# Moving an inverse square root from POOL to ScalarE in a fused attention-and-MLP kernel, with later weight loads, deeper input buffers and every engine in emission order

## The chip, the cores and the metric

One core of one Trainium2 chip. The metric is device microseconds of one execution. The kernel before took 673.85 us, the median of 3 runs (670.53 to 674.61).

## The reference, cut to what matters

```python
# q, k, v: (8 batches, 12 heads, 448 rows, 64)
def rmsnorm(x, g):
    return x / np.sqrt(np.mean(x * x, -1, keepdims=True) + 1e-06) * g
scores = np.matmul(rmsnorm(q, g_q), rmsnorm(k, g_k).transpose(0, 1, 3, 2)) / 8
attn = softmax(scores);  x = np.matmul(attn, v)        # to (3584, 768)
h = x @ w_in                                            # (3584, 2048)
out = (h * np.clip(h + 3, 0, 6) / 6) @ w_out            # (3584, 768)
```

The change concerns the inverse square root inside `rmsnorm`, one value per row and head, and the order of everything around it.

## The kernel before

Two heads form a pair, so there are 48 pairs P, six per batch. Each head's 448 rows are 384 rows plus a remainder of 64; the remainders of q and k of two batches are prepared together, at batches 0, 2, 4 and 6. A pair is loaded, prepared (squares, sums, inverse root, scaling), transposed on PE, scored, and multiplied by v. The MLP of a batch follows one batch later (h) and two batches later (y), so that PE always has something to mix in. The pools `ps_...` hold tiles of PSUM, the memory that PE writes its results to; one such tile is called a bank here.

```python
def rstd_of(ssq, n):                                   # inverse root, on POOL
    nc.gpsimd.tensor_scalar(ms[:], ssq, 1.0 / D, 1e-6, A_MULT, A_ADD)
    nc.gpsimd.tensor_tensor(out=rs[:], in0=ms[:], in1=npow[:, 0:n], op=A_POW)

def prep_pair(P):
    nc.gpsimd.tensor_tensor(out=sq[:], in0=qk_flat, in1=qk_flat, op=A_MULT)
    nc.vector.tensor_reduce(out=ssq[:], in_=sq..., axis=AX_X, op=A_ADD)
    rs = rstd_of(ssq[:], 4 * NT)
    for i in range(2):
        nc.gpsimd.tensor_tensor(out=qks[:, i]..., in0=qk[:, i]..., in1=rs..., op=A_MULT)
    nc.gpsimd.tensor_copy(out=va..., in_=vf...)

def prep_rest(b):                                      # remainder of batches b, b + 1
    for i in range(2):                                 # q, then k
        nc.gpsimd.tensor_tensor(out=sq[:], in0=src, in1=src, op=A_MULT)
        nc.vector.tensor_reduce(out=ssq[:], ...)
        rs = rstd_of(ssq[:], H)
        nc.gpsimd.tensor_tensor(out=qks[:, i], in0=qkr[:, i], in1=rs..., op=A_MULT)
# ... cut ...
ps_T = pool("ps_T", 1, space=PSUM)    # all transposes
ps_S = pool("ps_S", 3, space=PSUM)    # scores
ps_M = pool("ps_M", 2, space=PSUM)    # h and y share two banks
# ... cut ...
def att_items(P):                     # one attention step; fn's are called in this order
    items = [(0.0, lambda: load_step(P + 4)), (0.0, lambda: prep_step(P + 3)),
             (0.36, lambda: trans_step(P + 2))]
    # then scores of P+1 mixed with the v products of P, then the transpose of x
def h_items(G):                       # a group of 6 matmuls in two halves
    return [(c, lambda f=f, p=p: h_part(G, f, p)) for f in range(NFT) for p in range(2)]
# after half 2: ReLU on ScalarE, gating on VectorE; then the bank is free
```

Before, a scheduler arranges the recorded instructions on each engine. "Emission order" below means that each engine's instructions stay in the order in which the program calls them.

Of the kernel before, what the change touches and what calls it, by code (L numbers as in the profile page):

```python
# [10 lines left out]
BF16 = mybir.dt.bfloat16  # L11
A_MULT = mybir.AluOpType.mult
A_ADD = mybir.AluOpType.add
A_POW = mybir.AluOpType.pow
A_MIN = mybir.AluOpType.min
EXP = mybir.ActivationFunctionType.Exp
RELU = mybir.ActivationFunctionType.Relu
AX_X = mybir.AxisListType.X
# [4 lines left out]
def kernel(  # L23
# [33 lines left out]
    gq_t = const.tile([128, 1], FP32, name="gq_t")  # L57
    gk_t = const.tile([128, 1], FP32, name="gk_t")
    for a in range(2):
        nc.sync.dma_start(out=gq_t[a * 64:(a + 1) * 64, :], in_=g_q.rearrange("(p o) -> p o", o=1))  # L60
        nc.sync.dma_start(out=gk_t[a * 64:(a + 1) * 64, :], in_=g_k.rearrange("(p o) -> p o", o=1))
    mask = const.tile([128, 2], FP32, name="mask")
    nc.gpsimd.memset(mask[:], 0.0)
    nc.gpsimd.memset(mask[0:64, 0:1], 1.0)
# [1 line left out]
    gprime = const.tile([128, 1], FP32, name="gprime")  # L66
    nc.vector.tensor_mul(gprime[:], gq_t[:], gk_t[:])
    gmask = const.tile([128, 2], FP32, name="gmask")
    nc.vector.tensor_scalar(gmask[:], mask[:], gprime[:], 1.0 / 8.0, A_MULT, A_MULT)
    half_c = const.tile([128, 1], FP32, name="half_c")  # L70
    nc.gpsimd.memset(half_c[:], 0.5)
    zero_c = const.tile([128, 1], FP32, name="zero_c")
    nc.gpsimd.memset(zero_c[:], 0.0)
    npow = const.tile([128, 24], FP32, name="npow")
    nc.gpsimd.memset(npow[:], -0.5)

    w_in_sb = const.tile([128, NKT, DFF], BF16, name="w_in_sb")
    w_out_sb = const.tile([128, NFT, DM], BF16, name="w_out_sb")
# [17 lines left out]
        vbd_ring.append(t)  # L96


    qk_pool = pool("qk_pool", 4)
    v_pool = pool("v_pool", 3)  # L100
    sq_pool = pool("sq_pool", 2)
    st_pool = pool("st_pool", 4)
    qks_pool = pool("qks_pool", 4)
# [19 lines left out]
    st = {}  # L123


    def rstd_of(ssq, n):
        ms = st_pool.tile([128, n], FP32, name="ms", tag="ms")
        nc.gpsimd.tensor_scalar(ms[:], ssq, 1.0 / D, 1e-6, A_MULT, A_ADD)  # L128
        rs = st_pool.tile([128, n], FP32, name="rs", tag="rs")
        nc.gpsimd.tensor_tensor(out=rs[:], in0=ms[:], in1=npow[:, 0:n], op=A_POW)  # L130
        return rs

    def load_pair(P):
        b, j = divmod(P, NPAIR)
# [11 lines left out]
    def prep_pair(P):  # L146
        qk, vf = st.pop(("qk", P)), st.pop(("vf", P))
        sq = sq_pool.tile([128, 4 * NT * D], FP32, name="sq", tag="sq")
        qk_flat = qk[:].rearrange("p a h x -> p (a h x)")
        nc.gpsimd.tensor_tensor(out=sq[:], in0=qk_flat, in1=qk_flat, op=A_MULT)  # L150
        ssq = st_pool.tile([128, 4 * NT], FP32, name="ssq", tag="ssq")
        nc.vector.tensor_reduce(  # L152
            out=ssq[:], in_=sq[:].rearrange("p (n d) -> p n d", d=D), axis=AX_X, op=A_ADD)
        rs = rstd_of(ssq[:], 4 * NT)
        rs4 = rs[:].rearrange("p (a h t) -> p a h t", a=2, h=2)
        qks = qks_pool.tile([128, 2, NT, 2, D], BF16, name="qks")
        for i in range(2):
            nc.gpsimd.tensor_tensor(  # L158
                out=qks[:, i].rearrange("p t h d -> p h t d"),
                in0=qk[:, i].rearrange("p h (t d) -> p h t d", d=D),  # L160
                in1=rs4[:, i].unsqueeze(3).to_broadcast([128, 2, NT, D]),
                op=A_MULT)
        va = va_ring[P % NVA]
        nc.gpsimd.tensor_copy(
            out=va[:, :, :, 0:D], in_=vf[:].rearrange("p h (t d) -> p h t d", d=D))
        st["qks", P] = qks
        st["va", P] = va


    def load_rest(b):  # L170
        qkr = rst_pool.tile([128, 2, H, D], FP32, name="qkr")
        for i, src in enumerate((q, k)):
            for e in range(2):
                nc.sync.dma_start(  # L174
                    out=qkr[e * 64:(e + 1) * 64, i],
                    in_=src[b + e, :, SM:S, :].rearrange("h p d -> p h d"))
        st["qkr", b] = qkr
# [8 lines left out]
    def prep_vrest(b):  # L186
        vr = st.pop(("vr", b))
        vbd = vbd_ring[b % NVB]
        for a in range(2):
            nc.gpsimd.tensor_scalar(  # L190
                vbd[:, :, a * E1:a * E1 + D], vr[:], mask[:, a:a + 1], None, A_MULT)
        st["vbd", b] = vbd

    def prep_rest(b):
        qkr = st.pop(("qkr", b))
        qks = rst_pool.tile([128, 2, H, D], BF16, name="qkrs")
        for i in range(2):
            sq = sq_pool.tile([128, 4 * NT * D], FP32, name="sqr", tag="sq")
            src = qkr[:, i].rearrange("p h d -> p (h d)")
            nc.gpsimd.tensor_tensor(out=sq[:], in0=src, in1=src, op=A_MULT)  # L200
            ssq = st_pool.tile([128, H], FP32, name="ssqr", tag="ssq")
            nc.vector.tensor_reduce(
                out=ssq[:], in_=sq[:].rearrange("p (n d) -> p n d", d=D), axis=AX_X, op=A_ADD)
            rs = rstd_of(ssq[:], H)
            nc.gpsimd.tensor_tensor(  # L205
                out=qks[:, i], in0=qkr[:, i],
                in1=rs[:].unsqueeze(2).to_broadcast([128, H, D]), op=A_MULT)
        st["qkrs", b] = qks
# [44 lines left out]
    def score(P, u):  # L253
        b, j = divmod(P, NPAIR)
        if u == 0:
            st["e", P] = e_pool.tile([128, NU, S], BF16, name="eT")
        if u < 2 * NT:
            a, t = UNITS[u]
            lhsT = st["kp", P][:, a, t * 128:(t + 1) * 128]
        else:  # L260
            lhsT = st["kbd", b][:, j, :]
        ps = ps_S.tile([128, S], FP32, name="s_ps")
        nc.tensor.matmul(out=ps[:], lhsT=lhsT, rhs=st["qT", b][:, j, :], start=True, stop=True)  # L263
        nc.scalar.activation(out=st["e", P][:, u, :], in_=ps[:], func=EXP, bias=zero_c[:], scale=1.0)  # L264
# [117 lines left out]
    def h_items(G):  # L382
        c = 3 * ncol(G) / 2400
        return [(c, lambda f=f, p=p: h_part(G, f, p)) for f in range(NFT) for p in range(2)]
# [5 lines left out]
    def merge(*lists):  # L390
        totals = [sum(c for c, _ in l) or 1.0 for l in lists]
        done = [0.0] * len(lists)
        at = [0] * len(lists)
        res = []
        while True:
            live = [i for i in range(len(lists)) if at[i] < len(lists[i])]
            if not live:
                return res
            i = min(live, key=lambda i: (done[i] + lists[i][at[i]][0] / 2) / totals[i])
            c, fn = lists[i][at[i]]  # L400
            at[i] += 1
            done[i] += c
            res.append((c, fn))
# [4 lines left out]
    def load_step(P):  # L408
        if P >= NP:
            return  # L410
        b, j = divmod(P, NPAIR)
        load_pair(P)
        if j == 0:
            if b % 2 == 0:
                load_rest(b)
            load_vrest(b)

    def prep_step(P):
        if P >= NP:
            return  # L420
        b, j = divmod(P, NPAIR)
        prep_pair(P)
        if j == 0:
            if b % 2 == 0:
                prep_rest(b)
            prep_vrest(b)

    def trans_step(P):
        if P >= NP:
            return  # L430
        b, j = divmod(P, NPAIR)
        trans_pair(P)
        if j == 0 and b % 2 == 0:
            trans_rest(b)

    def att_items(P):
        b, j = divmod(P, NPAIR)
        n = P + 1
        items = [(0.0, lambda: load_step(P + 4)), (0.0, lambda: prep_step(P + 3)),
                 (0.36, lambda: trans_step(P + 2))]  # L440
        sc = [(0.19, lambda u=u: score(n, u)) for u in range(NU)] if n < NP else []
        vs = [(0.3, lambda t=t: av(P, t)) for t in range(NT + 1)]
        items += merge(sc, vs)
        items.append((0.18, lambda: xtrans(P)))
        if b % 2 == 1 and j % 3 == 2:
            items.append((0.18, lambda: xtrans_rest(b, j - 2)))
        return items

    for P in range(4):
        load_step(P)  # L450
    for kt in range(NKT):
        nc.gpsimd.dma_start(out=w_in_sb[:, kt, :], in_=moe_w_in[kt * 128:(kt + 1) * 128, :])
    for P in range(3):
        prep_step(P)
    for ft in range(0, NFT, 4):
        nc.gpsimd.dma_start(
            out=w_out_sb[:, ft:ft + 4, :],
            in_=moe_w_out[ft * 128:(ft + 4) * 128, :].rearrange("(f p) n -> p f n", p=128))
    for P in range(2):
        trans_step(P)  # L460
    for u in range(NU):
        score(0, u)

    for b in range(B):
        att = []
        for j in range(NPAIR):
            att += att_items(b * NPAIR + j)
        mlp = merge(h_items(b - 1) if b >= 1 else [], y_items(b - 2) if b >= 2 else [])
        for _, fn in merge(att, mlp):
            fn()  # L470
    for _, fn in merge(h_items(B - 1), y_items(B - 2)):
        fn()
    for _, fn in y_items(B - 1):
        fn()


# [28 lines left out]
```

## Time and profile before

The stretches below come from the table of windows. Its columns are the stretch, its length, the busy microseconds (and instructions) of PE, PE's weight loads, VectorE (DVE), ScalarE (ACT) and POOL, then PE's granted clock (1.00 is full speed), the mean share of the DMA engines, and GB/s.

```profile
0.00:33.60 33.60, 0.00 (x0) 0.00 (x0) 3.68 (x11) 0.00 (x0) 12.75 (x29) 1.00 0.97 193
33.60:200.00 166.40, 85.39 (x714) 52.57 (x715) 62.86 (x143) 63.53 (x113) 151.84 (x144) 0.80 0.41 98
200.00:500.00 300.00, 245.80 (x1939) 144.14 (x1938) 122.88 (x268) 147.80 (x261) 173.57 (x168) 0.92 0.24 70
500.00:600.00 100.00, 97.83 (x822) 58.69 (x820) 41.73 (x97) 65.19 (x115) 19.51 (x24) 1.00 0.12 39
```

PE does nothing for the first 33.6 us. Then POOL is busy for 91% of the time while PE is half busy at a mean clock of 0.80. From 200 us PE is busy for 82%, and only in the last stretch shown is it busy nearly all the time (98%).

Two groups of POOL's instructions (count, then busy microseconds and mean nanoseconds of one, then POOL's idle time before them):

```profile
L130 POOL TENSOR_TENSOR rs<-ms,npow 128x12 f32<-128x12 f32 x56 | 127.3, 2274 | 3.2
L150 POOL TENSOR_TENSOR sq<-qk 128x768 f32<-128x768 f32 x48 | 70.4, 1466 | 108.3 <-DMA qk<-in_k_dram 107.8
```

The power costs 2274 ns although it works on 12 elements per partition. The squares wait 107.8 us for loads.

From the list of waits of VectorE and of PE (who waited for whom: microseconds, times, longest):

```profile
DVE ssq L152 <- POOL sq L150: 170.8, 44, 11.2
...
PE t_ps L241 <- POOL qks L158: 51.8, 9, 36.1
PE xt_ps L329 <- DVE xn L291: 41.2, 14, 7.0
PE h_ps L349 <- DVE gT_1655 L356: 11.7, 3, 5.2
```

PE waits for the scaled q and k (36.1 of the 51.8 us are the start) and for VectorE's normalised x; in 23 of these 41.2 us VectorE, by its timeline, stood at a sum `ssq` that waited for POOL's squares. Waits of h on gating, over all tiles, add to 43.5 us.

### The profile page before, as it was taken

How to read it: one execution, taken by the hardware profiler on the slowest of the kernel's cores; microseconds unless marked ns; L12 is line 12 of the kernel's file. 1: busy time of each engine (PE TensorE's matmuls, PEld its weight loads, DVE VectorE, ACT ScalarE, POOL GpSimd, SP SyncE). 2: the span in 40 equal slices, each digit the busy share in tenths (PEclk: the TensorE clock that was granted, in tenths of full speed). 3: DMA queues.
4: the chain of work that ended last, by engine and by line, in shares of the span. 5: the costliest groups of instructions: out<-in, count | busy, mean ns of one | idle time of the engine just before them, and what ended most of it. 6: DMA issues, size and time to landing. Idle time of an engine off the chain costs nothing.

```text
span 672.3 us, 9839 instructions
## 1 busy us (share of the span) xinstructions
PE 493.8 (73%) x3848; PEld 290.1 (43%) x3848; DVE 245.9 (37%) x544; ACT 295.9 (44%) x521; POOL 357.7 (53%) x362
## 2 busy tenths in 40 slices
PE   0026354742869767978788868797879999999997
PEld 0013133421545434545454434464545556664454
DVE  0124223533645424334334423334444443433210
ACT  0006142531546434554345335464556666653321
POOL 2499699999796766546355684646455210000000
PEclk9999675877889978998789779999999999999999
DMA  8919733323331331222131212131222110101012
GB/s 154 232 43 198 147 100 85 93 59 83 89 83 49 93 90 53 86 79 61 58 83 49 71 47 71 59 95 60 84 59 71 48 37 25 36 24 36 24 47 72
DMA packets 69647, 50.98 MB, mean 76 GB/s; under 512 B 22752, under 2 KB 68832, under 8 KB 69600
## 3 DMA queue, kind: packets, MB, share of 16 engines
q1 hardware_dynamic: 66624, 44.06, 23.6%
q0 software_dynamic: 2976, 6.29, 5.2%
q8 instruction: 30, 0.49, 0.3%
q14 instruction: 17, 0.14, 0.1%
HBM read 45.61 MB, written 11.01 MB: 84 GB/s over the span
## 4 chain that ended last, share of the span: by engine, by line
POOL 35%; PE 30%; DMA 13%; DVE 8%; SPq 5%; issue 4%; ACT 3%; POOLq 0%; ACTq 0%
PE h_ps L349 13%; DMA qk<-in_k_dram 12%; PE y_ps L366 11%; POOL rs L130 11%; POOL sq L150 10%; POOL qks L158 8%; DVE ssq L152 4%; SPq L174 3%; PE s_ps L263 2%; ACT t_sb L354 2%; PE t_ps L241 2%; SPq L138 1%; POOL qkrs L205 1%; POOL ms L128 1%; DMA vr<-in_v_dram 1%
## 5 line engine op out<-in xcount | busy, mean ns | idle before, releaser
L264 ACT ACTIVATE eT<-s_ps,zero_c 128x448 bf16<-128x448 f32 x336 | 200.7, 634 | 117.9 <-PE s_ps L263 113.6
L354 ACT ACTIVATE t_sb<-h_ps,half_c 128x384 f32<-128x384 f32 (+1 forms) x128 | 81.0, 634 | 140.6 <-PE h_ps L349 136.2
L130 POOL TENSOR_TENSOR rs<-ms,npow 128x12 f32<-128x12 f32 x56 | 127.3, 2274 | 3.2
L150 POOL TENSOR_TENSOR sq<-qk 128x768 f32<-128x768 f32 x48 | 70.4, 1466 | 108.3 <-DMA qk<-in_k_dram 107.8
L349 PEld LDWEIGHTS <-w_in_sb 128*128 128x128 bf16 x768 | 75.0, 102 | 109.4 <-issue 70.6
L263 PE MATMUL s_ps<-qT,kp 128*128 128x448 bf16 x288 | 101.8, 384 | 9.5 <-DVE kp L247 4.3
L152 DVE TENSOR_REDUCE ssq<-sq 128x12 f32<-128x768 f32 x48 | 45.7, 951 | 170.8 <-POOL sq L150 170.8
L158 POOL TENSOR_TENSOR qks<-qk,rs 128x384 bf16<-128x384 f32 x96 | 77.5, 828 | 25.5 <-PE t_ps L241 24.6
L272 PEld LDWEIGHTS <-eT 128*128 128x128 bf16 x1152 | 69.1, 103 | 36.1 <-issue 8.5
L241 PE MATMUL t_ps<-identity,qks 128*128 128x128 bf16 x288 | 28.5, 240 | 68.6 <-POOL qks L158 51.8
L241 PEld LDWEIGHTS <-qks 128*128 128x128 bf16 x288 | 22.3, 107 | 80.4 <-POOL qks L158 54.2
L372 ACT COPY y_sb<-y_ps 128x384 f32<-128x384 f32 x56 | 26.8, 479 | 65.2 <-PE y_ps L366 65.1
L329 PE MATMUL xt_ps<-identity,xn 128*128 128x128 bf16 x144 | 19.1, 245 | 41.2 <-DVE xn L291 41.2
L263 PEld LDWEIGHTS <-kp 128*128 128x128 bf16 x288 | 29.3, 105 | 26.2 <-issue 7.9
L349 PE MATMUL h_ps<-xT_990,w_in_sb 128*128 128x512 bf16 x96 | 29.3, 423 | 12.2 <-DVE gT_1655 L356 11.7
L329 PEld LDWEIGHTS <-xn 128*128 128x128 bf16 x144 | 12.2, 109 | 53.9 <-DVE xn L291 47.4
L247 DVE TENSOR_SCALAR kp<-t_ps,gmask 128x384 bf16<-128x384 bf16 x96 | 35.2, 408 | 0.0
L349 PE MATMUL h_ps<-xT_2600,w_in_sb 128*128 128x512 bf16 x96 | 29.2, 420 | 6.9 <-DVE gT_3402 L356 6.4
L243 DVE COPY qT<-t_ps 128x384 bf16<-128x384 bf16 x48 | 17.0, 355 | 45.6 <-PE t_ps L241 45.4
L349 PE MATMUL h_ps<-xT_422,w_in_sb 128*128 128x384 bf16 x96 | 26.6, 376 | 7.1 <-DVE gT_905 L356 7.1
L349 PE MATMUL h_ps<-xT_1771,w_in_sb 128*128 128x384 bf16 x96 | 24.1, 363 | 9.8 <-DVE gT_2479 L356 9.6
L366 PE MATMUL y_ps<-w_out_sb,gT_1655 128*128 128x384 bf16 x128 | 29.1, 345 | 0.0
(102 smaller groups left out, 765.5 us busy)
## 6 DMA issues: line engine op xcount, KB each, us to landing
qk<-in_q_dram SPq DMA_DIRECT2D x48, 192.0 KB, 2.5
qk<-in_k_dram SPq DMA_DIRECT2D x48, 192.0 KB, 2.7
vf<-in_v_dram SPq DMA_DIRECT2D x48, 192.0 KB, 2.5
out_dram<-y_sb SPq DMA_DIRECT2D x48, 192.0 KB, 2.2
w_in_sb<-in_moe_w_in_dram POOLq DMA_DIRECT2D x6, 512.0 KB, 11.6
w_out_sb<-in_moe_w_out_dram POOLq DMA_DIRECT2D x4, 768.0 KB, 11.0
qkr<-in_q_dram SPq DMA_DIRECT2D x8, 192.0 KB, 3.8
qkr<-in_k_dram SPq DMA_DIRECT2D x8, 192.0 KB, 5.7
```

Of the source, the lines that this page charges most:

```text
L130: nc.gpsimd.tensor_tensor(out=rs[:], in0=ms[:], in1=npow[:, 0:n], op=A_POW)
L150: nc.gpsimd.tensor_tensor(out=sq[:], in0=qk_flat, in1=qk_flat, op=A_MULT)
L152: nc.vector.tensor_reduce(out=ssq[:], in_=sq[:].rearrange("p (n d) -> p n d", d=D), axis=AX_X, op=A_ADD)
L158: nc.gpsimd.tensor_tensor(out=qks[:, i].rearrange("p t h d -> p h t d"), in0=qk[:, i].rearrange("p h (t d) -> p h t d", d=D), in1=rs4[:, i ...
L241: nc.tensor.transpose(ps[:, i, t, :], qks[:, i, t].rearrange("p h d -> p (h d)"), identity[:])
L247: nc.vector.tensor_scalar_mul(kp[:, a, :], ps[:, 1].rearrange("p t c -> p (t c)"), gmask[:, a:a + 1])
L263: nc.tensor.matmul(out=ps[:], lhsT=lhsT, rhs=st["qT", b][:, j, :], start=True, stop=True)
L264: nc.scalar.activation(out=st["e", P][:, u, :], in_=ps[:], func=EXP, bias=zero_c[:], scale=1.0)
L272: nc.tensor.matmul(out=dst[:, a * E1:(a + 1) * E1], lhsT=eT[:, u, c0:c0 + 128], rhs=va[:, a, t, :], start=(first and a == 0 and t == 0), s ...
L349: nc.tensor.matmul(out=h_ps[:, 0:n], lhsT=w_in_sb[:, kt, f * 128:(f + 1) * 128], rhs=st["xT", G][:, kt, :], start=(kt == 0), stop=(kt == N ...
L354: nc.scalar.activation(out=t_sb[:, 0:n], in_=h_ps[:, 0:n], func=RELU, bias=half_c[:], scale=1.0 / 6.0)
L366: nc.tensor.matmul(out=y_ps, lhsT=gT[:, f, i * 128:(i + 1) * 128], rhs=w_out_sb[:, f, nh * HALF:(nh + 1) * HALF], start=(f == 0), stop=(f ...
```

## The change

Its intent: take the power off POOL (Ln and Exp on ScalarE, both from a table set loaded once), start earlier (weights after the first pairs, first squares on ScalarE, first remainder loads and the gains' loads on ScalarE's queue), load further ahead, and fix the order of each engine to the order of the program (emission order). The root is now exp(-0.5 ln(sum + 64e-6)), 1/8 of the old value for q and for k, so the factor on the gains goes from 1/8 to 8.

```diff
-    gmask = ... gprime, 1.0 / 8.0
+    gmask = ... gprime, 8.0
+    nc.scalar.preload_act_table_set("natural_log_exp_and_others")
-    qk_pool = pool("qk_pool", 4);  v_pool = pool("v_pool", 3)
+    qk_pool = pool("qk_pool", 5);  v_pool = pool("v_pool", 4)
     def rstd_of(ssq, n):
-        nc.gpsimd.tensor_scalar(ms[:], ssq, 1.0 / D, 1e-6, A_MULT, A_ADD)
-        nc.gpsimd.tensor_tensor(out=rs[:], in0=ms[:], in1=npow[:, 0:n], op=A_POW)
+        nc.scalar.activation(out=rs[:], in_=ssq, func=LN, bias=eps_c[:])
+        nc.scalar.activation(out=rs[:], in_=rs[:], func=EXP, bias=zero_c[:], scale=-0.5)
+    def square(out, x, early):      # early: pairs 0 to 2 and the first remainder
+        nc.scalar.square(...) if early else nc.gpsimd.tensor_tensor(...)
-                nc.sync.dma_start(            # remainder loads
+                (nc.scalar if b == 0 else nc.sync).dma_start(
-        items = [(0.0, lambda: load_step(P + 4)), ...
+        items = [(0.0, lambda: load_step(P + 5)), ...
+    with tc.manual_schedule():      # everything below in emission order
-    for P in range(4): load_step(P)
-    (w_in loads)
+        for P in range(5): load_step(P)
     for P in range(3):
         prep_step(P)
-    (w_out loads)
+            if P == 1: load_w_in()  # load_w_out() when pair 6 is prepared
     # ... the loops over batches are the same
```

More of the change, by code (lines that the diff above doesn't have):

```diff
@@ L13 @@
 A_ADD = mybir.AluOpType.add
-A_POW = mybir.AluOpType.pow
 A_MIN = mybir.AluOpType.min
+LN = mybir.ActivationFunctionType.Ln
 EXP = mybir.ActivationFunctionType.Exp
@@ L59 @@
     for a in range(2):
-        nc.sync.dma_start(out=gq_t[a * 64:(a + 1) * 64, :], in_=g_q.rearrange("(p o) -> p o", o=1))
-        nc.sync.dma_start(out=gk_t[a * 64:(a + 1) * 64, :], in_=g_k.rearrange("(p o) -> p o", o=1))
+        nc.scalar.dma_start(out=gq_t[a * 64:(a + 1) * 64, :], in_=g_q.rearrange("(p o) -> p o", o=1))
+        nc.scalar.dma_start(out=gk_t[a * 64:(a + 1) * 64, :], in_=g_k.rearrange("(p o) -> p o", o=1))
     mask = const.tile([128, 2], FP32, name="mask")
@@ L68 @@
     gmask = const.tile([128, 2], FP32, name="gmask")
-    nc.vector.tensor_scalar(gmask[:], mask[:], gprime[:], 1.0 / 8.0, A_MULT, A_MULT)
+    nc.vector.tensor_scalar(gmask[:], mask[:], gprime[:], 8.0, A_MULT, A_MULT)
     half_c = const.tile([128, 1], FP32, name="half_c")
@@ L73 @@
     nc.gpsimd.memset(zero_c[:], 0.0)
-    npow = const.tile([128, 24], FP32, name="npow")
-    nc.gpsimd.memset(npow[:], -0.5)
+    eps_c = const.tile([128, 1], FP32, name="eps_c")
+    nc.gpsimd.memset(eps_c[:], D * 1e-6)
+    nc.scalar.preload_act_table_set("natural_log_exp_and_others")
     w_in_sb = const.tile([128, NKT, DFF], BF16, name="w_in_sb")
@@ L96 @@
         vbd_ring.append(t)
-    qk_pool = pool("qk_pool", 4)
-    v_pool = pool("v_pool", 3)
+    qk_pool = pool("qk_pool", 5)
+    v_pool = pool("v_pool", 4)
     sq_pool = pool("sq_pool", 2)
@@ L126, in rstd_of @@
     def rstd_of(ssq, n):
-        ms = st_pool.tile([128, n], FP32, name="ms", tag="ms")
-        nc.gpsimd.tensor_scalar(ms[:], ssq, 1.0 / D, 1e-6, A_MULT, A_ADD)
         rs = st_pool.tile([128, n], FP32, name="rs", tag="rs")
-        nc.gpsimd.tensor_tensor(out=rs[:], in0=ms[:], in1=npow[:, 0:n], op=A_POW)
-        return rs
+        nc.scalar.activation(out=rs[:], in_=ssq, func=LN, bias=eps_c[:])
+        nc.scalar.activation(out=rs[:], in_=rs[:], func=EXP, bias=zero_c[:], scale=-0.5)
+        return rs
+    def square(out, x, early):
+        if early:
+            nc.scalar.square(out=out, in_=x)
+        else:
+            nc.gpsimd.tensor_tensor(out=out, in0=x, in1=x, op=A_MULT)
     def load_pair(P):
@@ L149, in prep_pair @@
         qk_flat = qk[:].rearrange("p a h x -> p (a h x)")
-        nc.gpsimd.tensor_tensor(out=sq[:], in0=qk_flat, in1=qk_flat, op=A_MULT)
+        square(sq[:], qk_flat, P < 3)
         ssq = st_pool.tile([128, 4 * NT], FP32, name="ssq", tag="ssq")
@@ L163, in prep_pair @@
         va = va_ring[P % NVA]
-        nc.gpsimd.tensor_copy(
+        st["prep", P] = nc.gpsimd.tensor_copy(
             out=va[:, :, :, 0:D], in_=vf[:].rearrange("p h (t d) -> p h t d", d=D))
@@ L199, in prep_rest @@
             src = qkr[:, i].rearrange("p h d -> p (h d)")
-            nc.gpsimd.tensor_tensor(out=sq[:], in0=src, in1=src, op=A_MULT)
+            square(sq[:], src, b == 0)
             ssq = st_pool.tile([128, H], FP32, name="ssqr", tag="ssq")
@@ L426, in prep_step @@
             prep_vrest(b)
+        if P == NPAIR:
+            load_w_out()
     def trans_step(P):
@@ L438, in att_items @@
         n = P + 1
-        items = [(0.0, lambda: load_step(P + 4)), (0.0, lambda: prep_step(P + 3)),
+        items = [(0.0, lambda: load_step(P + 5)), (0.0, lambda: prep_step(P + 3)),
                  (0.36, lambda: trans_step(P + 2))]
@@ L447, in att_items, with load_w_in, load_w_out @@
         return items
-    for P in range(4):
-        load_step(P)
-    for kt in range(NKT):
-        nc.gpsimd.dma_start(out=w_in_sb[:, kt, :], in_=moe_w_in[kt * 128:(kt + 1) * 128, :])
-    for P in range(3):
-        prep_step(P)
-    for ft in range(0, NFT, 4):
-        nc.gpsimd.dma_start(
-            out=w_out_sb[:, ft:ft + 4, :],
-            in_=moe_w_out[ft * 128:(ft + 4) * 128, :].rearrange("(f p) n -> p f n", p=128))
-    for P in range(2):
-        trans_step(P)
-    for u in range(NU):
-        score(0, u)
-    for b in range(B):
-        att = []
-        for j in range(NPAIR):
-            att += att_items(b * NPAIR + j)
-        mlp = merge(h_items(b - 1) if b >= 1 else [], y_items(b - 2) if b >= 2 else [])
-        for _, fn in merge(att, mlp):
-            fn()
-    for _, fn in merge(h_items(B - 1), y_items(B - 2)):
-        fn()
-    for _, fn in y_items(B - 1):
-        fn()
+    def load_w_in():
+        for kt in range(NKT):
+            nc.gpsimd.dma_start(
+                out=w_in_sb[:, kt, :], in_=moe_w_in[kt * 128:(kt + 1) * 128, :])
+    def load_w_out():
+        for ft in range(0, NFT, 4):
+            nc.gpsimd.dma_start(
+                out=w_out_sb[:, ft:ft + 4, :],
+                in_=moe_w_out[ft * 128:(ft + 4) * 128, :].rearrange("(f p) n -> p f n", p=128))
+    with tc.manual_schedule():
+        for P in range(5):
+            load_step(P)
+        for P in range(3):
+            prep_step(P)
+            if P == 1:
+                load_w_in()
+        for P in range(2):
+            trans_step(P)
+        for u in range(NU):
+            score(0, u)
+        for b in range(B):
+            att = []
+            for j in range(NPAIR):
+                att += att_items(b * NPAIR + j)
+            mlp = merge(h_items(b - 1) if b >= 1 else [], y_items(b - 2) if b >= 2 else [])
+            for _, fn in merge(att, mlp):
+                fn()
+        for _, fn in merge(h_items(B - 1), y_items(B - 2)):
+            fn()
+        for _, fn in y_items(B - 1):
+            fn()
 _INS = ['q', 'k', 'v', 'g_q', 'g_k', 'moe_w_in', 'moe_w_out']
```

## The prediction

> **What bounds it now.** The page's first part: PE busy 494 us of 672 (73%), POOL 358, ACT 296, DVE 246. By stage (table of windows):
> - 0 to 33.6 us: PE 0. First transpose at 36.1, first score at 48.2 (timeline). The chain of waits: issue of the k/q remainder loads (13.2 + 3.0 us, DMA engines 97% busy), then POOL's squares, powers, scalings.
> - 33.6 to 200 us: POOL busy 152 of 166 us, PE 85; granted clock 0.66-0.83.
> - 200 to 500 us: PE 41 of 50 us. The chain is a loop: scaling frees the q/k buffer, the next load lands in 2.6 us, square 1.47, reduction 0.95, power 2.27, scaling 2 x 0.83. In the waits, VectorE's reduction waited 170.8 us for squares; POOL waited 107.8 for q/k loads.
> - From 500 us PE is 96-100% busy.
>
> **What PE must do.** My estimate: the matmuls stream 1.003 million columns; the last 128 y matmuls (384 columns) took 0.163 us each, so PE needs about 430 us at full clock. The rest is start, waits, low clock.
>
> **What the change does.**
> - Removes from POOL per pair the power (2.27) and scale (0.20), and early squares: about 145 of 358 us. A pair then costs POOL 3.6 us.
> - Adds Ln and Exp of 12 columns to ACT, 56 times. Estimate from 384 columns at 0.58 and 512 at 0.69: 0.27 us each, 30 us in all; ACT to about 330. The Trainium skill ("ScalarE activation tables: per-element evaluation and per-set limits", What a function is on this engine) says functions in one set need no switch; this trace has one load of 1.28 us, and I expect one again.
> - Weights wait until two pairs are prepared; remainder loads move to ACT's queue, which may block ACT until about 15 us. First score near 27 us.
> - Five q/k and four v buffers, loads five pairs ahead: the loop breaks; POOL's wait for loads nearly vanishes.
> - Emission order loses the scheduler's placement. In the built order, PE's other work between one h group's end and the next's start is 0.86 us on average, against 1.20 before; ReLU plus gating needs about 1.6 (tail: stalls of 0.2 us after 1.46 us of y work). h's waits for gating should grow from 44 us to 70-110.
>
> **Sum.** First score 27; six attention-only steps, ACT-bound (7 x 0.57 + 0.55 + about 0.9 for the reduction) 33; next batch 44; six full batches at 53.5 plus about 12 of stalls, 390; last h with y 42; last y 21; tail 4.5: about 560.
>
> Predicted **558 us**, range **520 to 602**. Chances: faster by over 2% 0.95, within 2% 0.03, slower 0.02.
>
> **Signs if right.** First score at 22-33 us; POOL about 210 us; ACT about 330; one table load; reductions waiting for squares under 30 us; h waiting on gating PE's largest wait; clock at least 0.95 after 100 us. The Trainium skill ("TensorE: Matmul & The Clock Gate", Why this matters for your kernels) asks for no PE gaps over about 3 us.
>
> **What would make it wrong.** (a) In-order engines stall more than counted, ACT's Ln holding up ready exponentials: near 600. (b) Short gaps coincide with a y buffer just freed, so h hardly stalls: near 510. (c) Weights arrive after the first h needs them (about 60 us), or ACT stays blocked by its DMA issues past 20 us: +10 to 20.

## The result

The changed kernel took 630.31 us (median of 4, 629.93 to 631.45) beside 674.23 us for the kernel before on the same chip: a ratio of 0.936, 95% interval 0.9321 to 0.9399. A ratio is the mean time of one kernel's runs over the mean of the other's in the same rounds, so it is not quite the ratio of the medians. Executions over 1.5% slower than the fastest of the same kernel are left out of the means. The kernel is faster, but 72 us slower than the 558 us predicted and outside the range.

The same stretches of the changed kernel (table of windows):

```profile
0.00:33.60 33.60, 5.91 (x30) 2.97 (x31) 9.53 (x25) 10.30 (x21) 17.05 (x36) 1.00 0.72 163
33.60:200.00 166.40, 119.46 (x1112) 73.44 (x1111) 81.27 (x182) 103.59 (x208) 79.57 (x87) 0.94 0.47 111
200.00:500.00 300.00, 241.62 (x2000) 144.11 (x1998) 125.62 (x278) 169.92 (x329) 108.70 (x116) 0.96 0.28 76
500.00:600.00 100.00, 81.64 (x571) 45.64 (x571) 29.13 (x61) 40.18 (x72) 5.56 (x7) 1.00 0.08 25
```

The stretch from 33.6 to 200 us improved as foreseen: POOL's busy time nearly halved, and PE did 1112 matmuls where it had done 714. Between 200 and 500 us, however, PE did only 3% more matmuls (2000 against 1939), and from 500 to 600 us it is 82% busy where it had been 98%. (The last stretch does not hold the same work: before, it is nearly all of the last two batches; after, it is the last batch and most of the last h.)

Three of ScalarE's groups of instructions, as they are after the change:

```profile
L131 ACT ACTIVATE rs<-rs,zero_c 128x12 f32<-128x12 f32 x56 | 17.0, 304 | 1.8
L130 ACT ACTIVATE rs<-ssq,eps_c 128x12 f32<-128x12 f32 x48 | 14.6, 305 | 66.4 <-DVE ssq L159 66.4
L77 ACT ACT_TABLE_LOAD x1 | 1.3, 1283 | 3.3 <-issue 3.3
```

Ln and Exp together take 609 ns where POOL took 2274 for the power alone. The Trainium skill ("ScalarE: Activation LUTs", What ACT_TABLE_LOAD costs) gives about 280 ns plus 0.833 ns per element for an ACTIVATE with a pointer bias, from which I estimate 290 ns for 12 elements; the trace has 305 and 304.

The longest waits of PE and of ScalarE:

```profile
PE s_ps L270 <- ACT eT L271: 36.0, 13, 8.9
PE t_ps L248 <- POOL qks L165: 16.8, 2, 16.5
PE tr_ps L227 <- DVE kp L254: 14.7, 4, 8.5
PE h_ps L356 <- DVE gT_6673 L363: 13.9, 12, 1.5
...
ACT rs L130 <- DVE ssq L159: 66.4, 47, 6.5
...
ACT rs L130 <- DVE ssqr L209: 27.8, 8, 4.6
```

New is that the scores wait 36.0 us for ScalarE's exponentials (0.7 us before), with a longest wait of 8.9 us (three single waits of 8.1 to 8.9 us, one in each of the remainder steps described below, make 25.1 of the 36.0 us), and that ScalarE's Ln waits 27.8 us for the sums `ssqr`, which belong to the remainder. The waits of h on gating, over all tiles, are 52.3 us, against 43.5.

The stages, read from the timelines (a batch is taken to end where the normalisation of its last pair begins):

| stage | predicted us | measured us | difference |
|---|---|---|---|
| to the first score | 27 | 30.9 | +3.9 |
| six attention-only steps | 33 | 38.2 | +5.2 |
| next batch (attention and h) | 44 | 58.2 | +14.2 |
| six full batches | 390 | 417.9 | +27.9 |
| last h with y | 42 | 57.6 | +15.6 |
| last y, and the end | 25.5 | 25.4 | -0.1 |

Of the 44 steps after the first four, most last 9 to 13 us; six stand out, in three pairs: 16.2 and 14.0 us in the second batch, 20.7 and 15.3 in the fourth, 20.7 and 14.6 in the sixth. They are the steps in which the remainders of batches 2, 4 and 6 are prepared and transposed. ScalarE's timeline in the second of these places (start, duration, instruction, idle time before it and what ended that):

```profile
231.02 0.30 ACT L130 ACTIVATE rs<-ssq,eps_c 128x12 f32<-128x12 f32 x1 [1.75 <-DVE ssq L159]
231.35 0.30 ACT L131 ACTIVATE rs<-rs,zero_c 128x12 f32<-128x12 f32 x1
236.25 0.30 ACT L130 ACTIVATE rs<-ssqr,eps_c 128x12 f32<-128x12 f32 x1 [4.59 <-DVE ssqr L209]
236.59 0.30 ACT L131 ACTIVATE rs<-rs,zero_c 128x12 f32<-128x12 f32 x1
240.88 0.30 ACT L130 ACTIVATE rs<-ssqr,eps_c 128x12 f32<-128x12 f32 x1 [4.00 <-DVE ssqr L209]
241.22 0.30 ACT L131 ACTIVATE rs<-rs,zero_c 128x12 f32<-128x12 f32 x1
241.43 1.14 ACT L271 ACTIVATE eT<-s_ps,zero_c 128x448 bf16<-128x448 f32 x2
```

And PE's timeline in the same place:

```profile
230.51 0.35 PE L270 MATMUL s_ps<-qT,kp 128*128 128x448 bf16 x1
...
232.08 0.35 PE L270 MATMUL s_ps<-qT,kp 128*128 128x448 bf16 x1
232.27 0.65 PE L356 MATMUL h_ps<-xT_1759,w_in_sb 128*128 128x384 bf16 x3
232.76 0.35 PE L270 MATMUL s_ps<-qT,kp 128*128 128x448 bf16 x1
...
242.10 0.53 PE L270 MATMUL s_ps<-qT,kp 128*128 128x448 bf16 x1 [8.09 <-ACT eT L271]
243.68 1.12 PE L356 MATMUL h_ps<-xT_1759,w_in_sb 128*128 128x384 bf16 x3 [1.05 <-DVE gT_2461 L363]
```

Three scores began at 230.51, 232.08 and 232.76 and were done by 233.11, but ScalarE did not turn to them before 241.43: the remainder's two Ln stood in front, each waiting for a sum. (The sums waited 4.28 and 3.68 us for POOL, which first scaled the pair, and then scaled q between the squares of q and those of k.) All three score banks were full, so PE stood still for 8.09 us. The Trainium skill ("Perfetto Trace Analysis", Tensor Engine Instruction) says that ACT, DVE and GPSIMD are strict FIFO; this trace agrees, as the exponentials begin only after the second Ln and its Exp, 8.3 us after the last of the three scores was done. After the gap three h matmuls took 1.12 us instead of the usual 0.65: the skill's "TensorE: Matmul & The Clock Gate" (Why this matters for your kernels) says that a PE gap of over about 3 us lets the clock fall to half, and here it did: the granted clock recorded in the trace is 0.50 from 237.4 us, 3.4 us into the gap, to 247.6 us.

### The profile page after: what moved, and what is told of

It is laid out like the page before. It is cut to its first block, busy times and chain, and to the rows that moved or that the text cites. A ratio compares the mean times of both kernels' runs of the same rounds, so it can differ in the third digit from the quotient of the medians.

```text
span 628.2 us, 9751 instructions
## 1 busy us (share of the span) xinstructions
PE 471.6 (75%) x3848; PEld 279.5 (45%) x3848; DVE 246.9 (39%) x544; ACT 329.0 (52%) x638; POOL 210.9 (34%) x245
## 4 chain that ended last, share of the span: by engine, by line
PE 39%; ACT 15%; DVE 14%; issue 13%; POOL 10%; DMA 2%; SPq 1%; POOLq 0%; ACTq 0%
PE h_ps L356 15%; PE y_ps L373 15%; ACT t_sb L361 9%; PE s_ps L270 4%; ACT eT L271 4%; POOL sq L138 3%; POOL qks L165 2%; DVE ssq L159 2%; DVE gT_1643 L363 2%; PE x_ps L279 2%; DVE gT_3376 L363 2%; DVE gT_5109 L363 2%; DVE gT_6673 L363 1%; DMA qkr<-in_q_dram 1%; POOL sqr L138 1%
## 5 line engine op out<-in xcount | busy, mean ns | idle before, releaser
L356 PEld LDWEIGHTS <-w_in_sb 128*128 128x128 bf16 x768 | 72.1, 98 | 131.1 <-issue 93.6
L270 PE MATMUL s_ps<-qT,kp 128*128 128x448 bf16 x288 | 98.2, 370 | 36.0 <-ACT eT L271 36.0
L279 PEld LDWEIGHTS <-eT 128*128 128x128 bf16 x1152 | 64.0, 100 | 53.3 <-issue 25.1
L138 POOL TENSOR_TENSOR sq<-qk 128x768 f32<-128x768 f32 x45 | 66.2, 1470 | 0.0
L248 PE MATMUL t_ps<-identity,qks 128*128 128x128 bf16 x288 | 25.2, 225 | 35.7 <-POOL qks L165 16.8
L130 ACT ACTIVATE rs<-ssq,eps_c 128x12 f32<-128x12 f32 x48 | 14.6, 305 | 66.4 <-DVE ssq L159 66.4
L248 PEld LDWEIGHTS <-qks 128*128 128x128 bf16 x288 | 20.7, 100 | 47.2 <-issue 25.1
L356 PE MATMUL h_ps<-xT_6054,w_in_sb 128*128 128x512 bf16 x96 | 25.8, 378 | 15.1 <-DVE gT_6673 L363 13.9
L356 PE MATMUL h_ps<-xT_2582,w_in_sb 128*128 128x512 bf16 x96 | 25.9, 378 | 11.0 <-DVE gT_3376 L363 10.5
L356 PE MATMUL h_ps<-xT_986,w_in_sb 128*128 128x512 bf16 x96 | 25.9, 378 | 11.0 <-DVE gT_1643 L363 10.5
L356 PE MATMUL h_ps<-xT_4315,w_in_sb 128*128 128x512 bf16 x96 | 25.9, 378 | 11.0 <-DVE gT_5109 L363 10.5
L363 DVE SCALAR_TENSOR_TENSOR gT_6673<-t_sb,h_ps 128x512 bf16<-128x512 f32 x16 | 11.0, 688 | 44.5 <-ACT t_sb L361 44.5
L296 DVE RECIPROCAL rd<-x_ps 128x6 f32<-128x6 f32 x48 | 9.3, 194 | 47.3 <-PE x_ps L282 47.2
L298 DVE TENSOR_TENSOR xn<-x_ps,rd 128x384 bf16<-128x384 f32 x48 | 26.8, 557 | 1.6
## 6 DMA issues: line engine op xcount, KB each, us to landing
w_in_sb<-in_moe_w_in_dram POOLq DMA_DIRECT2D x6, 512.0 KB, 11.2
```

The lines of the kernel that those rows point to most:

```text
L138: nc.gpsimd.tensor_tensor(out=out, in0=x, in1=x, op=A_MULT)
L248: nc.tensor.transpose(ps[:, i, t, :], qks[:, i, t].rearrange("p h d -> p (h d)"), identity[:])
L270: nc.tensor.matmul(out=ps[:], lhsT=lhsT, rhs=st["qT", b][:, j, :], start=True, stop=True)
L279: nc.tensor.matmul(out=dst[:, a * E1:(a + 1) * E1], lhsT=eT[:, u, c0:c0 + 128], rhs=va[:, a, t, :], start=(first and a == 0 and t == 0), s ...
L356: nc.tensor.matmul(out=h_ps[:, 0:n], lhsT=w_in_sb[:, kt, f * 128:(f + 1) * 128], rhs=st["xT", G][:, kt, :], start=(kt == 0), stop=(kt == N ...
L363: nc.vector.scalar_tensor_tensor(out=st["gT", G][:, f, :], in0=t_sb[:, 0:n], scalar=1.0, in1=h_ps[:, 0:n], op0=A_MIN, op1=A_MULT)
```

## The experiments

Each kernel ran beside the kernel before on the same chip, in 3 rounds; the median of the kernel before was 672.9 to 676.9 us. All gave correct results. Differences in microseconds below are of medians, mostly from different chips; differences of the ratios give values up to 4 us apart from them. The diffs are cut, and text in brackets or after # stands for code left out. "Theory A" is that the remainder's chain, emitted as one block, holds ScalarE's and VectorE's queues; "theory B" is that in emission order h waits for its own bank.

### e1_rest_split: the remainder's sums earlier

```diff
-    def prep_rest(b):  # square, sum, Ln, Exp, scale for q; then the same for k
+    def sum_rest(b):   # squares and sums of q and k; emitted in the middle of the step before
+    def prep_rest(b):  # Ln, Exp, Ln, Exp, then scale, scale; where it was
```

> The changed kernel with one edit: the remainder's squares and sums of batches 2, 4, 6 are emitted half a step earlier, so that its two Ln/Exp follow each other with their sums ready. Same loads, same instructions. Theory A (the remainder's chain square-sum-Ln-Exp-scale, emitted as one block, holds ScalarE's and VectorE's queues for 9 us three times, and PE then idles 8 us and falls to half clock): the six long steps (16.2, 14.0, 20.7, 15.3, 20.7, 14.6 us) fall to 10 to 13 us each, time 585 to 600. Rival R (those steps are long because the remainder's loads of 256-byte rows come late): nothing changes, 625 to 633.

Measured: 612.22 us (611.78 to 613.88), ratio 0.9044 (0.9002 to 0.9086). The direction of theory A, half of its size. The first long step of each place fell (the last two from 20.7 to 10.8 and 10.9 us), the second did not (15.0 to 16.4 us). PE's wait in the scores for exponentials fell from 36.0 to 11.0 us. So the Ln in front of ready exponentials was one part of the block. The loads are the same, so rival R falls for this part.

### c1_rest_spread: and the remainder's transposes apart

```diff
 (e1, and)
-        if j == 0 and b % 2 == 0: trans_rest(b)          # 6 + 6 transposes behind the pair's 6
+        items.insert(2 * len(items) // 3, (0.3, lambda: trans_rest(tb, (1,))))   # k
+        items.insert(len(items) // 3, (0.3, lambda: trans_rest(tb, (0,))))       # q
```

> As e1_rest_split, and the remainder's transposes of q and of k are emitted at one and two thirds of the step instead of back to back behind the pair's. e1 took the two long steps of each block from 36 us to 26, against 20 of the same steps in the last batch. Theory A (the rest of the block is PE waiting, in its own order, for VectorE to empty the one transpose bank twice): the 15 to 16.4 us steps fall to 10 to 12, time 592 to 605. Rival: the 15 us come from POOL's extra 5.4 us of remainder scaling in the step before; then no change, 609 to 616.

Measured: 601.16 us (600.81 to 603.07), ratio 0.8915 (0.8886 to 0.8944). The second long steps fell to 11.0 to 12.2 us. All three sets of transposes use one PSUM bank, and PE, in order, had waited for VectorE to empty it between them: before the remainder's transposes it waited 12.2 us for VectorE in e1 and 4.3 us here. Together the block cost 29 us (630.31 to 601.16). ScalarE's wait for the remainder's sums:

```profile
ACT rs L130 <- DVE ssqr L208: 0.5, 1, 0.5
```

It was 27.8 us. The six full batches now take 394.0 us, against 390 predicted and 417.9 measured.

### e5_h_whole: an h group in one piece

```diff
-        return [(c, lambda f=f, p=p: h_part(G, f, p)) for f in range(NFT) for p in range(2)]
+        return [(2 * c, lambda f=f: (h_part(G, f, 0), h_part(G, f, 1))) for f in range(NFT)]
```

> The changed kernel (emission order kept) with each h group emitted whole (6 matmuls) instead of in two halves among other work. The work standing between one h group's end and the next one's start rises from 0.86 us on average to 1.91. Theory B (h waits for its bank because too little stands between): h's waits for gating fall from about 52 us to under 25, time 595 to 612. Rival: those waits hide other stalls (ScalarE's queue) that take their place, 622 to 632.

Measured: 593.96 us (591.86 to 594.11), ratio 0.8813 (0.8767 to 0.8859), a little below the range given for theory B, which holds. An h group needs a bank that the last group's gating has just left, as the other bank is mostly y's. With all other work standing between whole groups, little of the wait is left:

```profile
PE h_ps L356 <- DVE gT L363: 7.3, 14, 0.8
```

(52.3 us in the changed kernel.) Part of it moved: the pairs' transposes waiting for the evacuation of x rose from 17 to 31 us.

### e4_tail_banks: three banks for the last h

```diff
-            st["h"] = ps_M.tile([128, 512], FP32, name="h_ps", tag="M")
+            if G == B - 1:   # the scores are done by then
+                st["h"] = ps_S.tile([128, 512], FP32, name="s_ps", tag="S")
 # (else as before; the scores' tiles get the same size and tag)
```

> The changed kernel with the last batch's h tiles in the three PSUM banks of the scores, which are free by then. Theory B (in emission order h waits for its own bank, because only one of two is free beside an open y tile; the last h/y phase took 57.3 us against 43.2 before): that phase falls to 38 to 44 us and the whole to 612 to 619. Rival: ScalarE and VectorE limit that phase, nothing changes, 627 to 633.

Measured: 612.1 us (610.52 to 612.84), ratio 0.9042 (0.8993 to 0.909). The last h/y phase took 38.8 us (57.6 before this edit). PE's timeline there, first of the changed kernel, then of this one, where h's tiles bear the scores' name `s_ps`:

```profile
557.11 0.81 PE L373 MATMUL y_ps<-w_out_sb,gT_5927 128*128 128x384 bf16 x4
558.69 0.81 PE L356 MATMUL h_ps<-xT_6054,w_in_sb 128*128 128x512 bf16 x3 [0.77 <-DVE gT_6673 L363]
...
562.29 0.81 PE L356 MATMUL h_ps<-xT_6054,w_in_sb 128*128 128x512 bf16 x3 [1.50 <-DVE gT_6673 L363]
```

```profile
558.69 0.81 PE L359 MATMUL s_ps<-xT,w_in_sb 128*128 128x512 bf16 x3
559.34 0.81 PE L376 MATMUL y_ps<-w_out_sb,gT 128*128 128x384 bf16 x4
559.99 1.46 PE L359 MATMUL s_ps<-xT,w_in_sb 128*128 128x512 bf16 x6
```

With more banks there is no gap in front of h here, and h's waits for gating fall from 52.3 to 38.4 us, by just the 13.9 us of the last batch. So the bank was the limit there, not the speed of ScalarE or VectorE.

### e3_scheduler: everything but emission order

```diff
-    with tc.manual_schedule():
+    if True:
```

> The changed kernel without emission order: the scheduler places the instructions again, all else kept. Theory A says order costs stalls (52 us of h waiting for gating after 40 us, against 44 before, and the three remainder blocks), so without it 590 to 622. Rival O (emission order is what gained, the scheduler's greedy order is what delays attention): 640 to 670.

Measured: 585.86 us (584.11 to 588.76), ratio 0.8655 (0.8608 to 0.8701). That is just below theory A's range. As written, emission order costs 44 us on top of the other edits (630.31 less 585.86). The scheduler starts later (first score at 40.7 us instead of 30.9), but none of its steps after the first four is longer than 14.2 us, and its last h/y phase takes 43.6 us.

### b1_order_only: emission order alone on the kernel before

```diff
+    ctx.enter_context(tc.manual_schedule())
```

> The kernel before with emission order alone added. Theory A+: order by itself already breaks the load loop (in the order as written every load's buffer was freed two steps earlier), but gives it back in the remainder blocks and the h waits, so the sum is near nothing: 655 to 685, with POOL waiting for loads under 30 us (107.8 before). Rival O (order is the gain): under 645.

Measured: 669.63 us (669.05 to 670.41), ratio 0.9947 (0.9906 to 0.9988): the same. POOL's wait for q/k loads fell from 107.8 to 15.3 us. The sum hides a gain and losses of its size: the six attention-only steps take 30 us less, but the first score comes 11 us later, and the last h/y phase takes 14 us more. The remainder steps cost 20.5 and 16.0, 23.2 and 14.4, 23.2 and 15.3 us here too, this time with VectorE's sums as what stands in front.

### b2_buffers_only: buffers and prefetch alone on the kernel before

```diff
-    qk_pool 4, v_pool 3, load_step(P + 4), 4 pairs loaded first
+    qk_pool 5, v_pool 4, load_step(P + 5), 5 pairs loaded first
```

> The kernel before with five q/k buffers, four v buffers and loads five pairs ahead alone added, scheduler kept. If the load loop is what costs between 200 and 500 us (21 idle gaps of PE over 3 us, 95 us in all), 630 to 650. If POOL's own work and the scheduler's order are what holds PE, over 660.

Measured: 662.49 us (659.32 to 663.45), ratio 0.9832 (0.9784 to 0.988). Only 10 us, so little that the verdict is unclear (the interval reaches over 0.98). POOL's wait for loads here:

```profile
POOL sq L150 <- DMA qk<-in_k_dram: 47.2, 27, 15.0
```

More than half of the wait for loads is gone, and PE gained little: the wait for q/k buffers was not what held the kernel before. Part of it moved, as POOL now waits 63.8 us (24.6 before) for PE to be done with the scaled q and k.

### b3_lnexp_only: the inverse root alone on the kernel before

```diff
-    (POOL: scale, power)
+    (ScalarE: Ln, Exp; the table set pinned; the gain's factor 8)
```

> The kernel before with the inverse root on ScalarE (Ln, Exp) alone added, POOL's squares and everything else kept, scheduler kept. If the power on POOL is the main cost (chain shortened by 2.3 us in a loop of about 11), 600 to 630; if the loads' loop is, over 645.

Measured: 598.73 us, the median of three runs (595.27 to 603.3), ratio 0.8899 (0.883 to 0.8967). A fourth run, at 607.22 us, counts as slow and is left out. This single edit gives 74 us, more than the whole change. POOL's wait for loads in it:

```profile
POOL sq L151 <- DMA qk<-in_k_dram: 120.9, 33, 15.0
```

It is longer than before (107.8), and the kernel is 74 us faster. So this wait, the longest of POOL's, is here the idle time of an engine that has become fast enough, and it was the power that counted. The gain is spread: the first score comes 10 us earlier, the first two batches take 43 us less, the six full ones 22. The mean granted clock rose from 0.91 to 0.96; how much of the 74 us that is, no run separates.

### e2_pow_on_pool: the power back on POOL in the changed kernel

```diff
-        (ScalarE: Ln, Exp)
+        (POOL: scale, power; the gain's factor 1/8)
```

> The changed kernel with the inverse root back on POOL (scale 0.20 plus power 2.27 us), all else kept. Theory A: POOL has room in a 10.4 us step (3.6 + 2.5 = 6.1), so ordinary steps stay within 0.3 us; but the remainder's chain now holds VectorE's queue (its sums wait for POOL) about 12 us instead of 9, three times: 625 to 650. Rival P (the power on POOL was itself the bound, as POOL's 53 per cent and the chain of before suggest): every step grows by about 2.5 us, 48 x 2.5 = +120, 740 to 760.

Measured: 655.66 us (655.2 to 656.56), ratio 0.9683 (0.9639 to 0.9726). Close above theory A's upper end, far from rival P. Ordinary full steps are not longer (the six full batches take 415.2 us against 417.9), as with emission order POOL's 6.1 us fit in them. The cost is where POOL does not fit, in sum all of it before the full batches: attention-only steps take 7.2 us instead of 5.2, the first score comes at 35.0 us, and the first step of the remainder blocks takes 20.5 to 23.2 us instead of 16.2 to 20.7. I had counted only the last of these.

### c4_weights_early: weights at the start again

```diff
         for P in range(5): load_step(P)
+        load_w_in()                     # load_w_out() after the third pair is prepared
-                (nc.scalar if b == 0 else nc.sync).dma_start(
+                nc.sync.dma_start(
```

> The changed kernel with the weights' loads issued at the start as before and the remainder's first loads back on the sync queue; all else kept. Theory: the first score comes at 40 to 50 us instead of 30.9, part of which returns because the first h no longer waits for its weights: 638 to 652. Rival (weights held back only move the wait from the scores to the first h): 627 to 635.

Measured: 634.15 us (634.01 to 636.16), ratio 0.9405 (0.9375 to 0.9435). Inside the rival's range. The first score comes 7.4 us later (38.3 against 30.9), but the next six steps take 35.0 us instead of 38.2, so holding the weights back, with the move of the remainder's first loads, is worth 4 us. All later stages take the same time in both. The 3.2 us that come back are one step (11.2 us in the changed kernel, 7.9 here), and POOL's timeline of the changed kernel shows what lengthened it:

```profile
53.68 2.47 POOL L197 TENSOR_SCALAR vbd_97<-vr,mask 128x384 bf16<-128x384 f32 x2
56.10 3.09 POOL L465 DMA_DIRECT2D w_out_sb<-in_moe_w_out_dram  x4
59.17 1.52 POOL L138 TENSOR_TENSOR sq<-qk 128x768 f32<-128x768 f32 x1
```

It was not the weights' arrival: POOL issued the four loads of w_out, 3.09 us, in front of the next pair's squares; ScalarE's Ln waited 6.49 us for their sum, and PE 6.7 us for the exponentials behind that Ln. It is the remainder's mechanism once more.

### c2_order_all: the three repairs together

The edits of c1, e5 and e4.

> The changed kernel, emission order kept, with all three repairs: remainder spread, h whole, last h tiles in the scores' banks. If the three losses are what order costs and they add (about 35 to 45, 36 and 19 us, of which the last two overlap by about 8), 540 to 560, below the scheduler's 586. If repairing one lets the next wait take its place: 565 to 590.

Measured: 545.4 us (544.72 to 547.01), ratio 0.808 (0.8052 to 0.8108). The three gains add up almost exactly, 29, 36 and 18 us singly making 83, and together 85. By stage they do not: in the last h/y phase e5 and e4 gain 8 and 19 us, together only 18, while in the six full batches c1 and e5 gain 24 and 31, together 60. The exact sum is in part a coincidence. The first part of its page:

```profile
PE 455.8 (84%) x3848; PEld 278.4 (51%) x3848; DVE 247.2 (45%) x544; ACT 324.5 (60%) x638; POOL 210.7 (39%) x245
```

PE is busy for 84% of the span, against 75% in the changed kernel. This is the fastest version found, and it beats both kernels.

### c3_sched_all: the scheduler with h whole and three banks for the last h

```diff
 (c2 without the remainder's edits, and)
-    with tc.manual_schedule():
+    if True:
```

> e3_scheduler (no emission order) with h whole and the last h tiles in the scores' banks. The scheduler already moves work between h groups, so only the last phase should gain (43 us to 38): 574 to 586. If h waits there (28.9 us) also fall: 560 to 574.

Measured: 577.78 us (574.15 to 580.57), ratio 0.856 (0.8508 to 0.8612). The scheduler gains 8 us from these two edits, emission order 36 and 18: most of the 8 is the last h/y phase (43.6 to 37.9 us). The scheduler had already moved work into the other gaps, as h's waits for gating were 28.9 us under it (e3) and are 28.1 us here. Once the program's order is right, emission order is 32 us faster than this scheduled version, though the latter lacks the remainder's edits, so the two are not the same program.

## Why the prediction was wrong

- **Power off POOL: right.** POOL's busy time came to 210.9 us ("about 210"), ScalarE's to 329.0 ("about 330"), with one table load. The prediction gave this edit no figure of its own; alone it gives 74 us (b3), but only 25 us where all the other edits stand (e2).
- **The load loop: read wrongly, though it did not spoil the sum.** I put POOL's 107.8 us of waiting for loads among the bounds of the kernel before. Removing over half of it moved the time by 1.7%, a verdict of unclear (b2), and b3 is fast with 120.9 us of it. b1, where it nearly vanished and the time stayed the same, proves less, since the order's own losses stand against it.
- **Start: nearly right.** First score at 30.9 us, in the stated 22 to 33. The attention-only steps took 5.2 us more than "33"; 3.2 of them are one step, in which issuing the loads of w_out holds POOL (c4).
- **"Emission order loses the scheduler's placement": right in direction, wrong in what and how much.** I named one loss, h's waits for gating, "44 us to 70-110". In the trace these waits are 52.3 us, and h is indeed what PE waits for most. With the remainder's block repaired, the six full batches take 394.0 us against "390". That is in part luck: the single batches take 59.8 to 69.7 us where 65 were summed.
- **The step that failed: "six full batches at 53.5 plus about 12 of stalls, 390; last h with y 42", and "next batch 44" before it.** The sum had no term for the remainder. Its square, sum, Ln, Exp and scale, twice in a row and emitted as one block, held ScalarE's queue for about 9 us, and its transposes held PE's, three times: 29 us of the 72, by c1. The prediction's risk (a), "ACT's Ln holding up ready exponentials", was this mechanism, but it names neither the remainder nor a term for it, and allowed for it only "near 600". The pair's Ln costs less: with the block spread, PE's scores wait 11.1 us in all for exponentials. The last h with y was put at 42, close to the 43.6 us that it took before, where a scheduler had placed the instructions; in emission order it took 57.6 us, and the wait for a free bank explains it (e4: 38.8).
- **Clock: right on the mean, not throughout.** From 100 us on it is 0.97 ("at least 0.95"), but each remainder block takes the window of 50 us around it to 0.89 or 0.90.
- **Left open.** The second batch still takes 52.9 us with the block spread (c1), 9 us over my 44. Its granted clock there is 0.90, against 1.00 in the next batch, and PE waits 3.45 us for VectorE before the remainder's transposes and 2.96 us for a normalised x. No run separates these.

The comparison of the whole with its parts: Ln and Exp alone 0.890, buffers alone 0.983, order alone 0.995, all but order 0.866, all 0.936. The change contains a large gain and a loss of 44 us against the scheduler. Added to the kernel before, emission order lost nothing in sum (b1), because there it also gained.

## What to carry to other kernels

When engines run strictly in the order of the program, walk the order of each in-order queue past every rare block (remainders, first and last phases), not only through the ordinary step, and ask for each instruction that waits: what that is ready stands behind it? Issues of loads on an engine that computes are part of that walk too. Emit the parts of a dependent chain apart, so that each finds its input ready, and put the work that covers a buffer's turnaround between the groups that need the buffer. The longest wait of an engine is no bound by itself: test it by removing it.

## What the Trainium skill lacked or had wrong

- A power on POOL costs 2274 ns for 12 elements per partition (56 times, 127.3 us), more than a product of 768 elements at 1466 ns. "GPSIMD Engine Reference" has costs of additions, none of a power; on ScalarE Ln and Exp of the same took 609 ns.
- "Perfetto Trace Analysis" states the strict FIFO in a note on TensorE's timeline, without what it costs. Here an Ln that waited in front of ready exponentials stopped PE for 8.09 us, and moving such chains apart was worth 29 of 630 us.
- The same page (Optimizing Scalar/DVE Operations) advises breaking up ScalarE's or VectorE's instructions when these engines are not saturated but cause bubbles on others. No run here tried that, so this is no point against it. The section has nothing on mending such bubbles from PE's side: with ScalarE 52% busy and VectorE 39%, emitting six matmuls of h in one piece instead of two halves moved other work into the bank's turnaround and was worth 36 us (e5).
